# Attention and MLP on one core: the order of products within a group, the maxima of the first block, and the place of two small steps

## The chip, the core and the metric

The kernel runs on one core of one Trainium2 chip. The time is that of the device for one execution in microseconds, and the comparison is between medians of runs on the same chip. Five engines work side by side, each through its own queue in order: TensorE (PE, whose weight loads the profile lists as PEld), VectorE (DVE), ScalarE (ACT), GpSimd (POOL) and SyncE (SP), which here only issues DMA transfers. A transfer, once issued, runs by itself, but SP doesn't issue the next one before the one at the head of its queue has what it waits for.

## What is computed

```
h  = x + softmax((ln(x) wq)(ln(x) wk)^T / 4) (ln(x) wv) wo
h2 = h + silu(ln(h) w1) w2
```

One sequence of S = 2048 rows, D = 512, H = 32 heads of 16, F = 1792, all in float32. `ln` is a layer norm without gain or bias; the softmax runs over all 2048 keys.

## The kernel before

**Projections.** A first part makes the layer norm, the projections for q, k and v, and, beside them, the first row maxima of the scores. float32 products are made of two float16 halves of each operand, so the weights need scale factors. Their sums of squares are gathered on ACT (`square_rest`), reduced in `measure_rest`, and raised to the power -1/2 on POOL; `scale_of` turns each into a power of two on DVE. The factor for the attention output (`norms[:, 3:]`) goes its own way, in `set_output_factors`. Both this and `set_factors` are called when all projections are queued, just before the attention loop.

**Attention.** An item is four heads times a block of 512 queries: 32 items, eight to a block. A group is an item times 128 keys: 16 groups to an item, 512 in all, numbered g through the loop at the end of the kernel. A group has

- four scores (`scores`): a product of 64 rows, `ps<-qs,ks` in the profile, and an exponential on ACT, `pt<-ps`, into one of a ring of tiles;
- n maxima (`one_max`): a product of 48 rows, `ps<-ks,qs`, and a reduction on DVE, `mx<-ps`. They serve a later item: all 64 maxima of an item must be found, and its row maxima placed into `qs`, before its first score. They use a ring of three PSUM banks, so the fourth product waits for the first's reduction;
- the value products (`values`): four, `ps<-pt,va`, one for each head, of float32, in the four column parts of the array. They come at the end of a group and belong to an earlier one: two groups back, or one back where half products run.

Heads come in two kinds, j = 0 and j = 1, whose operands lie in partitions 0 to 63 or 64 to 127. A product of one kind and one of the other run on PE side by side: such a pair is called a slot here. Maxima may be of either kind, so they are chosen to fill the other half.

**Half products.** In 112 groups of each of blocks 1 to 3 (g = 146 to 257, 274 to 385, and from 402 on; the set `beside`) the MLP of the block before runs inside the attention groups. Each of its products, of 128 rows, is cut into two of 64 (`half_product`): an even group makes up to six halves of kind 0, the next, odd one the same six of kind 1, all in PSUM bank 3. To fit, an even group makes the kind 1 scores of itself and of the next group, and the odd one the kind 0 scores of both; so of the value products at the end of an odd group, which belong to the even group before, the second and the fourth use that odd group's first two exponentials. `beside_products` writes the order: a list for the half products' side (`same`) and one for the other (`other`), taken in turns. The first half product of a group gets a wait for an exponential of the group before (`fence`), since the two kinds write into one bank. When all halves of a product are in, `current["end"]` reads the bank on ACT.

**Output groups.** In the first item of blocks 1 to 3 (items 8, 16 and 24), groups c = 9 to 12 of the 16 (g = 137 to 140 in item 8) also multiply 128 finished rows by `wo`: twelve full products, with three maxima in the middle. Their rows then go through layer norm (DVE, POOL), are split in two (`split_normal`: ACT, then POOL or DVE) and turned by a DMA into `hts`, the operand of the first half products (`turn_beside`, `DMA_TRANSPOSE` on SP). These begin at group 146.

**How many maxima.** `maxima(g)` gives n: at most what the ring of `qs` tiles allows, and at least as many as the goals ask for, which are (how many maxima, by which group) for all later items. Groups with half products have four, five while they lag, three where a maximum is placed.

**Placing.** When an item's last maximum is found, `found_maxima` chooses. Far from the item's start (more than `FAR` groups) POOL finishes the maxima, and `CALM` groups later `place_far` turns them on DVE and sends them through DRAM (`md<-mt`, then `qs<-md`, which waits for it on SP). Nearer, `place_max` uses a transpose on PE, a copy on DVE and one transfer (`qs<-mn`).

Of the kernel before, what the change touches and what calls it, by code (L numbers as in the profile page):

```python
# [13 lines left out]
U32 = mybir.dt.uint32  # L14
# [14 lines left out]
NB = S // 512  # L29
# [35 lines left out]
AHEAD = 6  # L65

JOINT = 2
MORE = 3
FAR = 8
CALM = 4  # L70


OUTPUT = 8
# [16 lines left out]
def attention_mlp_kernel(ctx: ExitStack, tc: tile.TileContext, x, wqkv, wo, w1, w2, out):  # L90
# [12 lines left out]
    def pool(op, *a, **k):  # L103
        tc.keep_in_program_order(getattr(nc.gpsimd, op)(*a, **k))  # L104
# [15 lines left out]
    def dve(fn, *a, **k):  # L120
        pin(getattr(nc.vector, fn)(*a, **k))  # L121
# [417 lines left out]
    def scale_of(part, top):  # L539
        dve("tensor_scalar", sigma[:, part], norms[:, part], top, None, op0=ALU.mult)  # L540
        dve("tensor_scalar", sigma[:, part].bitcast(U32), sigma[:, part].bitcast(U32), 0x7F800000, None, op0=ALU.bitwise_and)
        dve("reciprocal", inverse[:, part], sigma[:, part])

    def set_output_factors():
        pool("tensor_scalar", norms[:, 3:], norms[:, 3:], 1e-30, None, op0=ALU.add)
        pool("tensor_tensor", norms[:, 3:], norms[:, 3:], expos[:, 3:], ALU.pow)
        scale_of(slice(3, 4), TOP / BOUND)
        for to, f in ((o_minus, -1.0), (o_twice, 2.0)):
            pool("tensor_scalar", to, o_s, f, None, op0=ALU.mult)

    def set_factors():
        scale_of(slice(3), TOP)
        for to, a, f in ((h_f, inverse[:, :1], 1 / LN), (g_s, w1_s, 1 / 32.0), (g_half, w1_s, 1 / 64.0),
                         (out_f, inverse[:, :1], 32.0)):
# [630 lines left out]
    def beside_products(g, n):  # L1185

        if not current:
            count, share, of, end = chains.pop(0)
            current.update(count=count, share=share, of=of, end=end, half=[0, 0], open=[], gone=0)
        side = g % 2  # L1190
        heads = [(x, k) for x in (g - side, g - side + 1) for k in range(4) if head(x, k)[1] != side]
        i, found, left = next_item(), [0, 0], [0, 0]
        if i < ITEMS:
            left = [len(todo[i, j]) for j in range(2)]
        count = current["count"] - current["half"][0] if side == 0 else current["half"][0] - current["half"][1]
        count = min(current["share"], count)
# [12 lines left out]
        if short > 0:  # L1209
            other[-1:-1] = [("none", 0)] * short  # L1210
        waiting = []
        for m in range(max(len(other), len(same))):
            for kind, x in same[m:m + 1] + other[m:m + 1]:
                if kind == "score":
                    waiting.append(scores(*x))
                    if len(waiting) < 4:
                        waiting[-1]()
# [4 lines left out]
        if current["half"][1] == current["count"]:  # L1222
            current["end"](space[:, 3, :])
            current.clear()
            waiting[3]()
        else:
            current["fence"] = waiting[3]()
# [30 lines left out]
    def finish_last(pending):  # L1258
# [85 lines left out]
        for f in range(FC):  # L1344
# [11 lines left out]
            if f > 1:  # L1356
# [6 lines left out]
    fixed = {**{8 * KC * b + c: 3 + MORE * (OUTPUT < c <= OUTPUT + 4) for b in range(1, NB) for c in range(2, KC + 2)},  # L1363
             **{g: 4 for g in beside}}
    before = [sum(n for x, n in fixed.items() if x < g) for g in range(groups + 1)]
    free = [sum(x not in fixed for x in range(g)) for g in range(groups + 1)]
# [1 line left out]
    def maxima(g):  # L1368
# [9 lines left out]
        goals += [(END - 32 * (1 - a), KC * LAST + HALF * a) for a in range(2) if KC * LAST + HALF * a > g]  # L1378
        rate = 0
        for n, start in goals:  # L1380
            end = max(g + 1, start - AHEAD)
# [4 lines left out]
            rate = min(rate, (ready - at["done"]) / (KC - 1 - c or KC))  # L1386
        at["due"] += rate
        if g < LAG:
            return 0
# [6 lines left out]
    set_output_factors()  # L1396
    set_factors()
    at["attention"] = True
    done = 0
    for g in range(groups):  # L1400
# [108 lines left out]
```

## Time and profile before

| | |
|---|---|
| runs | 1600.78 us median of 3 (1599.69 to 1601.96) |
| profiled execution | 1599.65 us; span 1597.8 us |
| mean granted clock of TensorE | 0.998 |
| PE busy | 1574.8 us (99%) |
| DVE busy | 1375.0 us (86%) |
| ACT busy | 1237.7 us (77%) |
| POOL busy | 565.1 us (35%) |

Times in the profile's rows count from the start of the span. The projections take 177.90 us, the groups before half products begin in block 1 end at 503.09, and the last group with half products ends near 1500. A row of the order of time has start, length, engine, line, operation, what it writes and reads, and a count where like rows are merged; line L97 is the helper through which every product goes, so groups are told apart by tiles. In brackets stands how long the engine was idle before it, and what ended that.

### The profile page before, as it was taken

What the parts mean: (1) busy time and instruction counts of PE and PEld (TensorE: products, weight loads), DVE (VectorE), ACT (ScalarE), POOL (GpSimd) and SP (SyncE); (2) the same over time, 40 slices, a digit from 0 to 9 for tenths busy, and PEclk for the clock granted to TensorE, in tenths of its full rate; (3) what the DMA queues carried; (4) which work ended last, traced back from release to release, by engine and by line L of the source; (5) the groups of instructions that cost most, each with busy time, mean ns of one, the idle gap of its engine ahead of it and who ended that gap; (6) DMA issues with size and microseconds to landing.
All of it is one profiled execution on the core that took longest, in us unless ns stands there. A gap on an engine that the chain in (4) does not pass through costs nothing.

```text
span 1597.8 us, 31074 instructions
## 1 busy us (share of the span) xinstructions
PE 1574.8 (99%) x11495; PEld 474.3 (30%) x11495; DVE 1375.0 (86%) x2211; ACT 1237.7 (77%) x2404; POOL 565.1 (35%) x803
## 2 busy tenths in 40 slices
PE   9999899999999999999999999999999999999999
PEld 6434222222222222222222222222222222222354
DVE  7999899999999999999999999999999999992232
ACT  6545699999987888877778888877768888878632
POOL 6643534544532454312142444310143444211100
PEclk9999999999999999999999999999999999999999
DMA  6667423333333122345433211444333121334332
GB/s 215 174 178 219 133 58 104 96 96 96 91 105 90 41 60 60 93 143 144 119 82 78 59 46 51 123 133 128 108 88 81 50 60 53 88 104 148 115 86 73
DMA packets 134403, 162.39 MB, mean 102 GB/s; under 512 B 41392, under 2 KB 78320, under 8 KB 134252
## 3 DMA queue, kind: packets, MB, share of 16 engines
q1 hardware_dynamic: 129500, 151.89, 34.0%
q10 hardware_dynamic: 4752, 8.52, 1.9%
q8 instruction: 90, 1.47, 0.4%
q14 instruction: 61, 0.50, 0.1%
HBM read 126.61 MB, written 24.76 MB: 95 GB/s over the span
## 4 chain that ended last, share of the span: by engine, by line
PE 90%; DVE 6%; ACT 2%; issue 1%; POOL 1%; POOLq 0%; DVEq 0%; ACTq 0%
PE ps L97 89%; DVE mx L307 3%; ACT pt L111 2%; PE ps L100 1%; DVE mx L305 1%; DVE ot L121 0%; DVE st L121 0%; DVE w L121 0%; DVE pvs L121 0%; POOL wv_l L104 0%; POOL sl L104 0%; DVE ks L121 0%; DVE xtl L121 0%; DVE mv L121 0%; POOL rs L104 0%
## 5 line engine op out<-in xcount | busy, mean ns | idle before, releaser
L307 DVE TENSOR_REDUCE mx<-ps 128x1 f32<-128x512 f32 x1842 | 1145.8, 683 | 87.0 <-PE ps L97 80.3
L111 ACT ACTIVATE pt<-ps 128x512 f32<-128x512 f32 x2048 | 1054.9, 605 | 206.3 <-PE ps L97 200.2
L97 PE MATMUL ps<-qs,ks 64*128 64x512 f16 x2048 | 685.2, 379 | 1.1 <-ACT pt L111 1.0
L97 PE MATMUL ps<-ks,qs 48*128 48x512 f16 x2048 | 628.3, 379 | 13.5 <-DVE mx L307 11.6
L97 PE MATMUL ps<-pt,va 128*17 128x512 f32 x4096 | 542.1, 599 | 1.0 <-DVE pvs L121 0.8
L97 PE MATMUL ps<-hts,w 64*128 64x512 f16 (+2 forms) x1212 | 283.6, 370 | 0.6 <-ACT pt L111 0.6
L97 PE MATMUL ps<-w,gates 64*128 64x512 f16 x1008 | 244.7, 376 | 0.5
L97 PEld LDWEIGHTS <-ks 64*128 64x128 f16 x2048 | 175.1, 94 | 200.2 <-issue 165.3
L97 PEld LDWEIGHTS <-qs 48*128 48x128 f16 x2048 | 146.8, 94 | 293.4 <-issue 281.4
L104 POOL TENSOR_TENSOR ri<-rc,minus 128x16 f32<-128x16 f32 x31 | 90.8, 2928 | 207.8 <-DMA rc<-dn 191.7
L97 PEld LDWEIGHTS <-w 64*128 64x128 f16 (+1 forms) x1212 | 114.0, 94 | 130.2 <-issue 34.5
L97 PEld LDWEIGHTS ps<-pt,va 128*17 128x17 f32 x4096 | 70.4, 95 | 237.5 <-issue 225.4
L97 PEld LDWEIGHTS <-gates 64*128 64x128 f16 x1008 | 92.3, 94 | 130.1 <-issue 28.6
L305 DVE TENSOR_REDUCE mx<-ps 128x2 f32<-128x1024 f32 x103 | 119.2, 1217 | 4.1 <-PE ps L97 3.5
L104 POOL TENSOR_SCALAR t<-t,factors 128x512 f32<-128x512 f32 x42 | 29.2, 695 | 196.9 <-ACT t L111 196.9
L111 ACT ACTIVATE g<-ps,factors 128x512 f32<-128x512 f32 x68 | 47.6, 700 | 42.7 <-PE ps L97 42.6
L104 POOL TENSOR_TENSOR ot<-ot,g 128x512 f32<-128x512 f32 x12 | 15.2, 1266 | 173.9 <-ACT g L111 173.9
L111 ACT ACTIVATE ks<-ps 128x512 f32<-128x512 f32 x30 | 17.9, 598 | 49.9 <-PE ps L97 42.9
L121 DVE SCALAR_TENSOR_TENSOR gh<-g,factors,gh 128x512 f16<-128x512 f32 x14 | 10.5, 751 | 52.1 <-ACT gh L111 52.1
L104 POOL TENSOR_TENSOR t<-t,g 128x512 f32<-128x512 f32 x42 | 53.5, 1275 | 3.5
L104 POOL TENSOR_TENSOR sl<-ks,sh 128x512 f16<-128x512 f32 x30 | 34.7, 1157 | 51.5 <-ACT sh L111 38.3
L104 POOL TENSOR_TENSOR gates<-t,gates 128x512 f16<-128x512 f32 x42 | 48.6, 1158 | 3.4
(161 smaller groups left out, 1019.0 us busy)
## 6 DMA issues: line engine op xcount, KB each, us to landing
w<-w2d SPq DMA_DIRECT2D x182, 256.0 KB
ks<-kd SPq DMA_DIRECT2D x120, 192.0 KB
w<-w1d SPq DMA_DIRECT2D x56, 256.0 KB
ks<-in_B_w_dram ACTq DMA_DIRECT2D x28, 256.0 KB
w<-in_B_w_dram SPq DMA_DIRECT2D x28, 256.0 KB
qs<-qd SPq DMA_DIRECT2D x128, 48.0 KB
kd<-sh SPq DMA_DIRECT2D x16, 256.0 KB
qd<-sh SPq DMA_DIRECT2D x16, 256.0 KB
```

The costliest lines, as they stand in the source:

```text
L97: return tc.keep_in_program_order(nc.tensor.matmul(*a, **k))
L100: tc.keep_in_program_order(nc.tensor.transpose(*a))
L104: tc.keep_in_program_order(getattr(nc.gpsimd, op)(*a, **k))
L111: ins = getattr(nc.scalar, fn)(*a, **k)
L121: pin(getattr(nc.vector, fn)(*a, **k))
L305: pin(nc.vector.tensor_reduce(of, space[:, n:n + 2, :], axis=AX.X, op=ALU.max))
L307: pin(nc.vector.tensor_reduce(of[:, j:j + 1], space[:, n, :], axis=AX.X, op=ALU.max))
```

## The change

Four things change together.

1. `beside_products` puts the half products first and maxima into every other slot of the other side; the fourth maximum comes seventh, beside the last score. The first half product of a group waits for the exponential that follows the last half, which in a full group is the third; before it was the fourth. Where there are few maxima, empty places keep the last score beside the last half.
2. `set_output_factors` is gone: the fourth factor is computed with the other three, and `set_factors` is called before the projection n = 18 of 0 to 19.
3. Of the four output groups only the first two have three more maxima (`MORE` is now a tuple). In the first block, goals beyond item 9 don't count, a group makes three maxima unless four are due, and groups with half products lag by another measure at the end.
4. `FAR` goes from 8 to 5 and `CALM` from 4 to 3, so that more items are placed through DRAM.

```diff
-MORE = 3
-FAR = 8
-CALM = 4
+MORE = 3, 3, 0, 0
+FAR = 5
+CALM = 3
...
-        pool("tensor_scalar", norms[:, :3], norms[:, :3], 1e-30, None, op0=ALU.add)
-        pool("tensor_tensor", norms[:, :3], norms[:, :3], expos[:, :3], ALU.pow)
+        pool("tensor_scalar", norms, norms, 1e-30, None, op0=ALU.add)
+        pool("tensor_tensor", norms, norms, expos, ALU.pow)
...
     def set_factors():
-        scale_of(slice(3), TOP)
+        dve("tensor_scalar", sigma[:, :3], norms[:, :3], TOP, None, op0=ALU.mult)
+        dve("tensor_scalar", sigma[:, 3:], norms[:, 3:], TOP / BOUND, None, op0=ALU.mult)
+        dve("tensor_scalar", sigma.bitcast(U32), sigma.bitcast(U32), 0x7F800000, None, op0=ALU.bitwise_and)
+        dve("reciprocal", inverse, sigma)
...
+            if n == 18:
+                set_factors()
...
-        other = [("max", 1 - side)] * found[1 - side]
-        other = [step for m, of in enumerate(heads) for step in [("score", of), *other[m:m + 1]]]
-        same = [("max", side)] * found[side]
-        same[1:1] = [("half", side)] * count
-        short = len(same) - len(other)
-        if short > 0:
-            other[-1:-1] = [("none", 0)] * short
+        other = [("score", of) for of in heads]
+        for m in range(found[1 - side]):
+            other.insert(2 * m if m < 3 else len(other), ("max", 1 - side))
+        same = [("half", side)] * count + [("max", side)] * found[side]
+        last = max(m for m, step in enumerate(other) if step[0] == "score")
+        if last < count - 1:
+            other[last:last] = [("none", 0)] * (count - 1 - last)
...
+                    if current.get("fence", True) is None:
+                        current["fence"] = weigh()
...
+                    if m == count - 1:
+                        current["fence"] = None
+                        if current["half"][1] == current["count"]:
+                            current["end"](space[:, 3, :])
+                            current.clear()
...
-            weave(project_rows(n, ps), {6: lambda: singles(MORE)})
+            weave(project_rows(n, ps), {6: lambda: singles(MORE[n])})
...
-            most = 4 - late_now + (64 + 4 * (g + LEAD) > at["done"])
+            most = 4 - late_now + (64 + 4 * (g + (LEAD if g < marks[-1] else 3)) > at["done"])
...
-        goals = [(64 * (n + 1), KC * n) for n in range(i + 1, LAST)]
+        goals = [(64 * (n + 1), KC * n) for n in range(i + 1, LAST) if g >= FIRSTS[0] * KC or n <= FIRSTS[0] + 1]
...
-        most = 2 if late_now or c == JOINT and 0 < i <= FIRSTS[0] else 4
+        most = 2 if late_now or c == JOINT and 0 < i <= FIRSTS[0] else 3 + (at["due"] >= 4 and i < FIRSTS[0])
```

**PE, end of group 160 and start of group 161.** In these rows a weight load of `w` opens a half product, of `qs` a maximum, of `ks` a score; `pt,va` are the value products. First the last slots of group 160, before:

```order
L97 LDWEIGHTS w
L97 MATMUL ps<-hts,w 128x512
L97 LDWEIGHTS qs_102
L97 MATMUL ps<-ks_101,qs_102 128x512
L97 LDWEIGHTS w
L97 MATMUL ps<-hts,w 128x512
L97 LDWEIGHTS ks_99
L97 MATMUL ps<-qs_100,ks_99 128x512
L97 MATMUL ps<-pt,va 17x512 x4
```

And now:

```order
L97 LDWEIGHTS w
L97 MATMUL ps<-hts,w 128x512
L97 LDWEIGHTS ks_99
L97 MATMUL ps<-qs_100,ks_99 128x512
L97 LDWEIGHTS qs_102
L97 MATMUL ps<-ks_101,qs_102 128x512
L97 LDWEIGHTS ks_99
L97 MATMUL ps<-qs_100,ks_99 128x512
L97 MATMUL ps<-pt,va 17x512 x4
```

The fourth maximum moved from the sixth slot to the seventh, and the third score took its place. Then the first slots of group 161, before:

```order
L97 LDWEIGHTS qs_102
L97 MATMUL ps<-ks_101,qs_102 128x512
L97 LDWEIGHTS ks_99
L97 MATMUL ps<-qs_100,ks_99 128x512
L97 LDWEIGHTS w
L97 MATMUL ps<-hts,w 128x512
L97 LDWEIGHTS qs_102
L97 MATMUL ps<-ks_101,qs_102 128x512
```

And now:

```order
L97 LDWEIGHTS w
L97 MATMUL ps<-hts,w 128x512
L97 LDWEIGHTS qs_102
L97 MATMUL ps<-ks_101,qs_102 128x512
L97 LDWEIGHTS w
L97 MATMUL ps<-hts,w 128x512
L97 LDWEIGHTS ks_99
L97 MATMUL ps<-qs_100,ks_99 128x512
```

A half product stands in the first slot beside a maximum, and the first score is in the second slot.

**DVE, around the start of the attention.** The ten maxima in the middle are those of the last two projections; the difference of the two orders:

```order
 L121 STREAM_TRANSPOSE mt<-ns 128x32
+L121 TENSOR_SCALAR factors<-norms 128x3
+L121 TENSOR_SCALAR factors<-norms 128x1
+L121 TENSOR_SCALAR factors<-factors 128x4
+L121 RECIPROCAL factors<-factors 128x4
 L307 TENSOR_REDUCE mx<-ps 128x1 x10
-L121 TENSOR_SCALAR factors<-norms 128x1
-L121 TENSOR_SCALAR factors<-factors 128x1
-L121 RECIPROCAL factors<-factors 128x1
-L121 TENSOR_SCALAR factors<-norms 128x3
-L121 TENSOR_SCALAR factors<-factors 128x3
-L121 RECIPROCAL factors<-factors 128x3
```

Four operations stand ahead of these maxima where six stood behind them. POOL's eight small operations on `factors` move with them, from behind the last projection's `sl<-ks,sh` to two projections ahead of it.

**SP, in the output groups of item 8.** The turns of finished rows (`hts<-g`) with what is queued around them, before:

```order
L131 DMA_TRANSPOSE hts<-g 128x8x128
L127 DMA ks_103<-kd 48x2048
L127 DMA w<-w1d 128x1024
L131 DMA_TRANSPOSE hts<-g 128x8x128
L127 DMA w<-w1d 128x1024
L131 DMA_TRANSPOSE hts<-g 128x8x128 x2
L127 DMA w<-w1d 128x1024
```

And now:

```order
L131 DMA_TRANSPOSE hts<-g 128x8x128
L127 DMA md<-mt 32x32 x4
L127 DMA qs_108<-md 2x1024 x2
L127 DMA ks_103<-kd 48x2048
L127 DMA w<-w1d 128x1024
L131 DMA_TRANSPOSE hts<-g 128x8x128
L127 DMA w<-w1d 128x1024
L131 DMA_TRANSPOSE hts<-g 128x8x128 x2
L127 DMA w<-w1d 128x1024
```

The placement of item 9, before a near one (`qs<-mn`, queued ahead of all turns), is a far one and stands between the first turn and the second. In all, 23 placements go through DRAM instead of 13 in the attention loop.

More of the change, by code (lines that the diff above doesn't have):

```diff
@@ L535, in measure_rest @@
         dve("tensor_reduce", norms[:, 2:3], ps[:, 28:n], axis=AX.X, op=ALU.add)
-        pool("tensor_scalar", norms[:, :3], norms[:, :3], 1e-30, None, op0=ALU.add)
-        pool("tensor_tensor", norms[:, :3], norms[:, :3], expos[:, :3], ALU.pow)
[L539 to L549, printed above, removed]
+        pool("tensor_scalar", norms, norms, 1e-30, None, op0=ALU.add)
+        pool("tensor_tensor", norms, norms, expos, ALU.pow)
     def set_factors():
-        scale_of(slice(3), TOP)
+        dve("tensor_scalar", sigma[:, :3], norms[:, :3], TOP, None, op0=ALU.mult)
+        dve("tensor_scalar", sigma[:, 3:], norms[:, 3:], TOP / BOUND, None, op0=ALU.mult)
+        dve("tensor_scalar", sigma.bitcast(U32), sigma.bitcast(U32), 0x7F800000, None, op0=ALU.bitwise_and)
+        dve("reciprocal", inverse, sigma)
         for to, a, f in ((h_f, inverse[:, :1], 1 / LN), (g_s, w1_s, 1 / 32.0), (g_half, w1_s, 1 / 64.0),
-                         (out_f, inverse[:, :1], 32.0)):
+                         (out_f, inverse[:, :1], 32.0), (o_minus, o_s, -1.0), (o_twice, o_s, 2.0)):
             pool("tensor_scalar", to, a, f, None, op0=ALU.mult)
@@ L1214, in beside_products @@
                 if kind == "score":
-                    waiting.append(scores(*x))
-                    if len(waiting) < 4:
-                        waiting[-1]()
+                    weigh = scores(*x)
+                    if current.get("fence", True) is None:
+                        current["fence"] = weigh()
+                    else:
+                        weigh()
                 elif kind == "max":
@@ L1221, in beside_products @@
                     half_product(x)
[L1222 to L1227, printed above, removed]
+                    if m == count - 1:
[3 more added lines that the diff above has]
+                            current.clear()
     found = {}
@@ L1362, in attention_mlp_kernel @@
     beside = {g for m in marks for g in range(m + 2, min(groups, m + 2 + 4 * FC + 4 * FC))}
-    fixed = {**{8 * KC * b + c: 3 + MORE * (OUTPUT < c <= OUTPUT + 4) for b in range(1, NB) for c in range(2, KC + 2)},
+    fixed = {**{8 * KC * b + c: 3 + (MORE[c - OUTPUT - 1] if OUTPUT < c <= OUTPUT + 4 else 0) for b in range(1, NB) for c in range(2, KC + 2)},
              **{g: 4 for g in beside}}
@@ L1374, in maxima @@
             at["due"] = 0
-            most = 4 - late_now + (64 + 4 * (g + LEAD) > at["done"])
+            most = 4 - late_now + (64 + 4 * (g + (LEAD if g < marks[-1] else 3)) > at["done"])
             return max(0, min(most, ready - at["done"]))
-        goals = [(64 * (n + 1), KC * n) for n in range(i + 1, LAST)]
-        goals += [(END - 32 * (1 - a), KC * LAST + HALF * a) for a in range(2) if KC * LAST + HALF * a > g]
+        goals = [(64 * (n + 1), KC * n) for n in range(i + 1, LAST) if g >= FIRSTS[0] * KC or n <= FIRSTS[0] + 1]
+        goals += [(END - 32 * (1 - a), KC * LAST + HALF * a) for a in range(2) if g >= FIRSTS[0] * KC and KC * LAST + HALF * a > g]
         rate = 0
@@ L1388, in maxima @@
         if g < LAG:
+            at["due"] = 0
             return 0
-        most = 2 if late_now or c == JOINT and 0 < i <= FIRSTS[0] else 4
+        most = 2 if late_now or c == JOINT and 0 < i <= FIRSTS[0] else 3 + (at["due"] >= 4 and i < FIRSTS[0])
         n = max(0, min(most, int(at["due"]), ready - at["done"]))
```

3 lines of the change are left out of this document (removed).

## The prediction

> **What bounds the kernel now.** I read the page's busy times, then the chain that ended last, then a table of stretches cut where the program changes its work, and last the order of time inside one group of each kind.
>
> ```profile
> PE 1574.8 (99%) x11495; PEld 474.3 (30%) x11495; DVE 1375.0 (86%) x2211; ACT 1237.7 (77%) x2404; POOL 565.1 (35%) x803
> PE 90%; DVE 6%; ACT 2%; issue 1%; POOL 1%; POOLq 0%; DVEq 0%; ACTq 0%
> ...
> 177.90:193.84 15.94, 11.22 (x65) 1.91 (x65) 10.69 (x23) 9.37 (x18) 10.11 (x20) 0.79 0.75 186
> 503.09:804.71 301.62, 300.92 (x2475) 84.50 (x2472) 278.74 (x455) 252.93 (x490) 101.33 (x154) 1.00 0.33 91
> ```
>
> The columns of the last two are length, then busy time (count) of PE, PEld, DVE, ACT, POOL, granted clock, DMA share, GB/s. They are groups 2 to 5, and the first 112 groups with half products (146 to 257; two more such stretches follow). PE is on the chain for 90%, so a group is worth what passes before PE reaches the next group's first product. In the first stretch PE is busy for 11.22 of 15.94 us at a clock of 0.79; in the other it is never free (300.92 of 301.62), so there the order of its products is all that can change.
>
> **Part 1: the factors move ahead of attention.** DVE, POOL and PE there, then a stretch:
>
> ```profile
> 171.22 6.23 DVE L307 TENSOR_REDUCE mx<-ps 128x1 f32<-128x512 f32 x10
> 181.60 0.15 DVE L121 TENSOR_SCALAR factors<-norms 128x1 f32<-128x1 f32 x1 [4.16 <-POOL norms L104]
> ...
> 179.44 1.16 POOL L104 TENSOR_TENSOR sl<-ks,sh 128x512 f16<-128x512 f32 x1 [2.30 <-issue]
> ...
> 183.81 0.58 PE L97 MATMUL ps<-ks,qs 48*128 48x512 f16 x1 [4.50 <-DVE mx L307]
> 184.31 1.91 PE L97 MATMUL ps<-pt,va 128*17 128x512 f32 x8
> ...
> 183.80:186.10 2.30, 2.29 (x9) 0.15 (x8) 1.74 (x3) 0.00 (x0) 0.34 (x2) 0.50 0.91 196
> ```
>
> DVE's six small operations stand in its queue ahead of the memset and of group 2's maxima, and wait 4.16 us for a power on POOL that stands behind the last projection's subtraction. PE has no free bank for its fourth maximum, idles 4.50 us, and then runs at half clock. In the new order the power is taken with the other three, three projections earlier, and DVE's four operations come ten maxima earlier. Group 2 then goes as fast as its last bank allows. I build it from group lengths below: its products to the fourth score about 1.0 us, the step to the value products 0.3, these 0.98, so 2.3; group 3 waits for late exponentials, 2.4; groups 4 and 5 take 1.96 each: 8.6 instead of 15.94, a gain of 7.3. Against it, four DVE operations of about 0.16 us now stand ahead of ten maxima that run without a gap from 171.22 to 177.45 and pace PE: 0.6 lost. POOL's eight small operations go between subtractions where it idles (2.30 us above). Net **-6.7** (-1.5 if something else fills the gap, -7.3 if the 0.6 is hidden).
>
> [...]
>
> **Part 2: fewer maxima in the first block.** Three groups of three maxima in a row, then one of four with the one behind it:
>
> ```profile
> 231.01:236.89 5.88, 5.88 (x49) 1.32 (x47) 5.61 (x10) 5.88 (x13) 3.48 (x8) 1.00 0.39 112
> 236.89:241.39 4.50, 4.34 (x35) 0.97 (x33) 4.42 (x8) 4.08 (x10) 2.44 (x3) 1.00 0.87 233
> ```
>
> A three costs 1.96; a four costs 4.50 - 2 x 1.96 = 0.58 more, as DVE then paces PE. In groups 6 to 136 the two orders have 28 and 20 fours (twos cost what threes cost): **-4.7** (-4.0 to -5.2).
>
> **Part 3: the third and fourth output group lose three maxima each.** Groups 139 and 140, the pairs 267-268 and 395-396, and group 397:
>
> ```profile
> 479.19:485.77 6.58, 5.67 (x36) 1.57 (x33) 6.16 (x13) 3.08 (x6) 3.02 (x4) 1.00 0.22 60
> 485.77:491.60 5.83, 5.58 (x35) 1.71 (x32) 5.67 (x12) 2.57 (x5) 1.90 (x3) 1.00 0.61 137
> 829.43:841.38 11.95, 10.95 (x65) 3.18 (x62) 11.10 (x22) 5.65 (x11) 4.93 (x7) 1.00 0.48 99
> 1182.78:1193.87 11.09, 10.80 (x64) 3.26 (x61) 10.51 (x21) 5.65 (x11) 4.93 (x7) 1.00 0.01 2
> 1193.87:1197.11 3.24, 2.33 (x20) 0.44 (x17) 3.21 (x8) 2.48 (x5) 0.75 (x2) 1.00 1.00 169
> ```
>
> Without the insert a group is a three (1.96) plus twelve full products at the 0.22 spacing shown below (2.6) plus a mode step, 4.75; DVE's 3.7 us of work hides beside it. Six groups at 4.75 are 28.5 against 12.41 + 11.95 + 11.09 = 35.45, so -6.95; group 138 now has six maxima instead of five, +0.25: **-6.7** (-5 to -8). Group 397 falls from four maxima to three; part of its 3.24 returns in the groups behind it: **-0.8**.
>
> **Part 4: a placement moves into SP's queue ahead of the turns.** SP's last two turns in the output groups, a far placement elsewhere, DVE's work before the place, and a late stretch:
>
> ```profile
> 496.07 2.97 SPq L131 DMA_TRANSPOSE hts<-g  x2
> ...
> 785.74 1.71 SPq L127 DMA_DIRECT2D md<-mt  x4
> 788.52 0.53 SPq L127 DMA_DIRECT2D qs<-md  x2
> ...
> 492.62 0.18 DVE L121 BATCH_NORM_AGGREGATE mv<-st 128x2 f32<-128x6 f32 x1
> ...
> 501.15:503.10 1.95, 1.95 (x21) 0.43 (x17) 1.73 (x4) 1.55 (x4) 0.00 (x0) 1.00 0.15 57
> ```
>
> The far placement is now queued in group 141, behind DVE's 492.8 in old time. SP writes `md` from 493.0, reads it back 2.78 later until 496.3, loads a key block and weights (about 1.1), and only then turns rows 1 to 3: 1.3, a load of 0.6, then 2.6, ending near 501.9 instead of 499.04. Up to now the turned rows had landed by about 501.2 (DMA share 0.15 from there on), 2.2 behind the last issue, and were needed at 503.09, where half products begin. Now they land near 504.0, and the need moves from the second slot to the first: 0.9 late in the first block. In the others groups before that point are slower by some tenths, so I take 0.5 each, **+1.5** (0 to +9). The PE transpose and copy of the old near placement (about 0.4 us of PE and DVE) go from these groups.
>
> **Part 5: groups with half products.** One even group and the next one's first rows, then its fourth maximum's DVE work and exponentials:
>
> ```profile
> 600.59 0.39 PE L97 MATMUL ps<-qs,ks 64*128 64x512 f16 x1
> 601.68 0.38 PE L97 MATMUL ps<-hts,w 64*128 64x512 f16 x1
> 601.76 0.37 PE L97 MATMUL ps<-ks,qs 48*128 48x512 f16 x1
> 601.90 0.38 PE L97 MATMUL ps<-hts,w 64*128 64x512 f16 x1
> 602.28 1.05 PE L97 MATMUL ps<-pt,va 128*17 128x512 f32 x8
> 603.26 0.39 PE L97 MATMUL ps<-ks,qs 48*128 48x512 f16 x1
> ...
> 601.01 0.69 DVE L307 TENSOR_REDUCE mx<-ps 128x1 f32<-128x512 f32 x1 [0.19 <-PE ps L97]
> ...
> 600.39 2.72 ACT L111 ACTIVATE pt<-ps 128x512 f32<-128x512 f32 x5
> 601.54 0.59 ACT L111 ACTIVATE pt<-ps 128x512 f32<-128x512 f32 x1
> ```
>
> The group takes 603.26 - 600.59 = 2.67. In slot five the maximum starts 0.08 behind its partner (601.76 against 601.68): with three banks it waits for the first maximum's reduction, which ended at 601.70. The delay runs on to the last score and the value products behind it. With maxima in slots 0, 2, 4 and 6 the fourth comes 0.22 later, the wait is gone, and an **even** group falls to about 2.60.
>
> In an **odd** group the value products belong to the group before, and two of their four `pt` are this group's first and second exponential. The second ended at 602.13, 1.54 into the group; the value products start at 1.69, so nothing waits. The scores now come one slot (0.23) later. What a wait costs, two groups show:
>
> ```profile
> 545.42 0.60 ACT L111 ACTIVATE pt<-ps 128x512 f32<-128x512 f32 x1
> 546.00 1.10 PE L97 MATMUL ps<-pt,va 128*17 128x512 f32 x8
> 547.04 0.39 PE L97 MATMUL ps<-ks,qs 48*128 48x512 f16 x1
> ...
> 1450.90 1.22 PE L97 MATMUL ps<-pt,va 128*17 128x512 f32 x8
> 1452.07 0.39 PE L97 MATMUL ps<-qs,ks 64*128 64x512 f16 x1
> 1452.50 2.06 ACT L111 ACTIVATE pt<-ps 128x512 f32<-128x512 f32 x4 [0.49 <-PE ps L97]
> 1454.62 0.39 PE L97 MATMUL ps<-qs,ks 64*128 64x512 f16 x1
> 1455.12 1.09 ACT L111 ACTIVATE pt<-ps 128x512 f32<-128x512 f32 x2 [0.55 <-PE ps L97]
> ```
>
> At 545.42 a copy had pushed the second exponential back; it ended at 546.02, the value products took 1.10 instead of 1.05, and the next group came 1.02 behind that end. The second case (1.22; next group 1.17 behind their start instead of 0.98) passes 0.17 of wait on in full. So an odd group takes the second exponential's end plus 1.02. From score to first exponential it is 0.46 in the full groups (a score behind a maximum), and behind a half product 0.43 (1452.07 to 1452.50) or 0.50 (1454.62 to 1455.12; there the group's start itself had waited for an exponential). Such waits for the group's start are hidden now, so I take 0.44, near the lower: end at 1.54 + 0.23 - 0.02 = 1.75, odd group 2.77. A pair costs 5.38 instead of 5.35, over 137 pairs **+4** (+2 at 0.43, +8 at 0.46, +19 at 0.50).
>
> Halves first, and their wait on the **third exponential**: I cost it at nothing. The fourth of the group at 600.59 ended at 603.11, only 0.15 before the next group's first slot; with scores a slot later it would end behind it. The third ends about 0.4 earlier and stays covered; without that cover each group would lose about 0.15. In the 18 remaining groups without maxima the last score still comes with the last half, so they keep the fourth.
>
> What the first block saved must be found later. Three groups of five:
>
> ```profile
> 1210.60:1219.75 9.15, 9.13 (x73) 2.51 (x70) 8.73 (x15) 6.72 (x13) 3.71 (x4) 1.00 0.33 85
> ```
>
> A five costs 3.05, 0.38 over 2.67, in either order, as its last maximum waits for the second's reduction. There are 27 instead of 17: **+3.8**. Four groups fewer run without maxima, +0.4; the 20 odd groups that a copy now delays by 0.05 lose that separate delay, -1.0.
>
> Sum: -6.7 - 4.7 - 6.7 - 0.8 + 1.5 + 4 + 3.8 + 0.4 - 1.0 = **-10.2 us**. The profiled execution took 1599.65 us (span 1597.8), 1.1 below the median 1600.78; I get 1589.5.
>
> **Rivals.**
> *The late second exponential wins (slower).* If the first exponential follows its score by 0.50, an odd group takes 2.83, and an even one 2.66, since its fourth score waits for the bank that this exponential frees. The pair costs 0.14 more, 19 instead of 4: 1604.5. It decides from 0.105 per pair. For it speaks the row at 1455.12, against it that most groups show 0.43 to 0.46. Chance 0.08.
> *The turns arrive late.* SP's queue costs 3 us at each of three starts, +9 instead of +1.5: 1597. For it speaks that `qs` waits for `md` with the turns behind it; against it the 1.9 us between 501.2 and 503.1. Chance 0.10.
> *The gap at the start stays in part*, the accumulator's memset or the late projections' copies on ACT taking over: -1.5 instead of -6.7, 1594.7. Chance 0.10.
> *The stall overlaps the next group.* If the next weights load while the fourth value product waits, 0.09 of each odd group's stall is hidden: 12 less, 1577.5. The case at 1450.90, which passed all on, speaks against it. Chance 0.08.
> [...]
>
> **How the numbers follow.** The forecast with its small terms (1585 to 1594) has 0.56, the four rivals 0.36, and 0.08 is left to mixtures. A change of 0.2% (3.2 us) is about what a measurement can tell. Faster: 0.56 + 0.08 + 0.10, half of the turns' 0.10, most of the rest: 0.84; same 0.07; slower 0.09. The range 1581 to 1598 takes in the forecast, the start's rival and half of the turns'.
>
> **What would show it.** Right: no PE idle time near 180 and a clock of 1.00 there; even groups near 2.60, odd near 2.77 with value products of about 1.2; output groups 139 and 140 near 4.75. Wrong: odd groups above 2.8; a wait of PE for `hts` at the first half product; a four that costs nothing once neighbours change.

## The result: 13.5 us slower, and the profile after

| | before | after |
|---|---|---|
| runs | 1600.26 us median of 4 (1599.69 to 1601.96) | 1613.72 us median of 4 (1612.78 to 1615.9) |
| ratio | | 1.0084, 95% interval 1.0067 to 1.0102 |
| span of the profiled execution | 1597.8 us | 1612.1 us |
| mean granted clock | 0.998 | 0.993 |

The forecast was 1589.5 (1581 to 1598), so it has the wrong sign. Busy times and the chain that ended last, on the page of after:

```profile
PE 1586.0 (98%) x11485; PEld 520.1 (32%) x11485; DVE 1377.2 (85%) x2199; ACT 1240.0 (77%) x2404; POOL 577.8 (36%) x861
PE 88%; DVE 8%; ACT 1%; DMA 1%; issue 1%; POOL 0%; SPq 0%; POOLq 0%; ACTq 0%; DVEq 0%
```

PE is busy 11 us longer for ten products fewer. Behind the stalls products ran at a lower clock (0.50 in groups 144, 272 and 400; 8 us more in the five groups of the table), and in groups with half products a value product that waits for its exponential counts as busy (1.22 us for the four at 705.71 below, 1.05 at 484.73; 12 us more there; elsewhere it is 9 less). With both traces cut at the starts of the same groups, each part of the change has its own stretch:

| stretch | before | after | difference | predicted |
|---|---|---|---|---|
| up to group 2 | 177.90 | 179.42 | +1.5 | +0.6 |
| groups 2 to 5 | 15.94 | 8.63 | -7.3 | -7.3 |
| groups 6 to 136 | 274.57 | 269.45 | -5.1 | -4.7 |
| output groups, three times four | 68.27 | 61.08 | -7.2 | -6.7 |
| **the five groups behind them, three times** | 36.38 | 55.25 | **+18.9** | +0.7 |
| groups with half products and to 510 | 902.2 | 916.0 | **+13.7** | +7.2 |
| groups 258 to 264 and 386 to 392, end | 122.5 | 122.3 | -0.2 | 0 |

The differences add up to +14.3, which is the difference of the spans. The stretches of after, in the columns of the prediction's first table (length, busy PE, PEld, DVE, ACT, POOL, granted clock, DMA share, GB/s): groups 2 to 5, group 139, groups 141 and 142, then 143, 144 and 145 by themselves, and the first 112 groups with half products:

```profile
179.42:188.05 8.63, 8.53 (x61) 1.88 (x62) 7.30 (x13) 8.43 (x18) 1.16 (x1) 1.00 0.60 141
468.38:473.12 4.74, 4.71 (x32) 1.61 (x29) 3.96 (x8) 3.08 (x6) 2.74 (x5) 1.00 0.01 3
477.86:482.48 4.62, 4.61 (x34) 0.87 (x30) 4.58 (x9) 4.20 (x9) 1.90 (x3) 1.00 0.02 2
482.48:488.27 5.79, 3.15 (x20) 0.61 (x17) 2.19 (x4) 1.50 (x4) 0.00 (x0) 1.00 0.88 216
488.27:493.07 4.80, 4.55 (x16) 0.57 (x16) 3.76 (x7) 3.66 (x7) 0.00 (x0) 0.50 0.50 110
493.07:495.95 2.88, 2.88 (x19) 0.59 (x16) 1.89 (x3) 2.06 (x4) 0.00 (x0) 0.65 0.00 0
495.95:805.24 309.29, 307.82 (x2486) 101.59 (x2483) 285.01 (x465) 253.66 (x488) 101.70 (x154) 1.00 0.32 89
```

The first two rows are as forecast: the gap at the start is closed at full clock, and an output group without maxima takes 4.74. The stall sits in group 143, where PE is busy 3.15 of 5.79 us; groups 144 and 145 then run at a clock of 0.50 and 0.65. What PE waited for is found by going back one engine at a time. PE and ACT in the order of time (start, length; in brackets the idle time before and what ended it):

```profile
480.71 2.10 ACT L111 ACTIVATE pt<-ps 128x512 f32<-128x512 f32 x4
484.73 1.05 PE L97 MATMUL ps<-pt,va 128*17 128x512 f32 x8
487.10 0.62 ACT L111 CAST g<-w 128x512 f16<-128x512 f32 x1 [4.29 <-DMA hts<-g]
488.27 0.58 PE L97 MATMUL ps<-qs,ks 64*128 64x512 f16 x1 [2.49 <-ACT pt L111]
```

PE waits for an exponential to free a score bank. ACT isn't short of scores. At the head of its queue stands the split of the last finished row (`g<-w`), and that waits 4.29 us for a turn (`hts<-g`) to end, because there are two buffers `g` and the turn reads the one that is wanted. SP's queue shows why the turn is late (two of the placement's four writes stand ahead of these rows):

```profile
480.02 0.88 SPq L127 DMA_DIRECT2D md<-mt  x2
482.04 0.52 SPq L127 DMA_DIRECT2D qs<-md  x2
482.60 0.31 SPq L127 DMA_DIRECT2D ks<-kd  x1
482.95 0.43 SPq L127 DMA_DIRECT2D w<-w1d  x1
483.42 1.25 SPq L131 DMA_TRANSPOSE hts<-g  x1
485.40 4.31 SPq L131 DMA_TRANSPOSE hts<-g  x2
```

The turn at 483.42 is row 1's. It stands behind the far placement and its reading back, and it is this turn that frees the buffer. One odd group with half products (from 704.04; the score, the first two exponentials, the value products, the next group), and the even group and the odd one as stretches:

```profile
704.27 0.38 PE L97 MATMUL ps<-qs,ks 64*128 64x512 f16 x1
704.76 1.08 ACT L111 ACTIVATE pt<-ps 128x512 f32<-128x512 f32 x2 [0.60 <-PE ps L97]
705.71 1.22 PE L97 MATMUL ps<-pt,va 128*17 128x512 f32 x8
706.86 0.39 PE L97 MATMUL ps<-w,gates 64*128 64x512 f16 x1
701.43:704.04 2.61, 2.61 (x23) 0.84 (x22) 2.28 (x5) 1.96 (x4) 0.00 (x0) 1.00 0.22 63
704.04:706.86 2.82, 2.82 (x26) 0.96 (x24) 2.69 (x5) 2.18 (x5) 0.00 (x0) 1.00 0.92 251
```

The second exponential ends at 705.84, and the next group comes 1.02 later, as forecast. But the first one starts 0.49 behind its score, not 0.44.

### The profile page after: what moved, and what is told of

It reads as the page before. It is cut to its first block, busy times and chain, and to the rows that moved or that the text cites. A ratio compares the mean times of both kernels' runs of the same rounds, so it can differ in the third digit from the quotient of the medians.

```text
span 1612.1 us, 31239 instructions
## 1 busy us (share of the span) xinstructions
PE 1586.0 (98%) x11485; PEld 520.1 (32%) x11485; DVE 1377.2 (85%) x2199; ACT 1240.0 (77%) x2404; POOL 577.8 (36%) x861
## 4 chain that ended last, share of the span: by engine, by line
PE 88%; DVE 8%; ACT 1%; DMA 1%; issue 1%; POOL 0%; SPq 0%; POOLq 0%; ACTq 0%; DVEq 0%
PE ps L97 87%; DVE mx L307 6%; DVE mx L305 1%; PE ps L100 1%; ACT pt L111 1%; DMA hts<-g 1%; ACT g L111 0%; POOL wv_l L104 0%; DMA w<-w2d 0%; SPq L127 0%; DVE pvs L121 0%; DVE g L121 0%; DVE st L121 0%; DVE ot L121 0%; DVE ks L121 0%
## 5 line engine op out<-in xcount | busy, mean ns | idle before, releaser
L97 PE MATMUL ps<-ks,qs 48*128 48x512 f16 x2048 | 680.4, 382 | 7.6 <-DVE mx L307 4.0
L97 PE MATMUL ps<-qs,ks 64*128 64x512 f16 x2048 | 644.4, 380 | 11.8 <-ACT pt L111 11.7
L97 PE MATMUL ps<-pt,va 128*17 128x512 f32 x4096 | 565.5, 601 | 0.5 <-DVE pvs L121 0.3
L97 PEld LDWEIGHTS <-qs 48*128 48x128 f16 x2048 | 169.2, 95 | 78.3 <-issue 35.3
L97 PEld LDWEIGHTS <-w 64*128 64x128 f16 (+1 forms) x1212 | 102.0, 95 | 236.8 <-ACT pt L111 105.6
L97 PEld LDWEIGHTS ps<-pt,va 128*17 128x17 f32 x4096 | 84.5, 95 | 221.3 <-issue 207.5
L97 PEld LDWEIGHTS <-gates 64*128 64x128 f16 x1008 | 82.1, 94 | 218.4 <-ACT pt L111 119.7
L104 POOL TENSOR_TENSOR mx<-mx 128x32 f32<-128x32 f32 x52 | 12.4, 239 | 109.2 <-DVE mx L307 102.6
```

What stands on the lines that cost most here:

```text
L97: return tc.keep_in_program_order(nc.tensor.matmul(*a, **k))
```

## Experiments

Medians are given beside those of the kernel before in the same comparison (1600.4 to 1601.1 us). "The five groups" are 141 to 145, 269 to 273 and 397 to 401.

### The stall: three buffers g

```diff
-zp.tile([P, 512], F32, name="g")
+zp.tile([P, 512], F32, name="g", bufs=3)
```

> The changed kernel with three buffers g instead of two, nothing else; SP's order stays as it is. Theory: ScalarE's 4.3 us wait for the buffer goes and with it the half clock, but the second to fourth turn still stand behind the far placement, so the first half products (group 146 and its like) may wait up to 2 us for turned rows: 4 to 6 us less in each of three blocks, 1596 to 1602 us. Rival 1: what stops the groups is SP's queue itself (the row maxima qs arrive late): ScalarE's wait goes, TensorE's stall stays, 1611 to 1614 us. Rival 2: the turned rows are covered after all: 1594 us, the same as with the near placement.

Measured: 1598.14 us, ratio 0.9985 (0.9975 to 0.9995). ACT no longer waits for a turn. The five groups as stretches, then two pieces of the chain in the third block:

```profile
477.64:490.43 12.79, 12.12 (x79) 2.35 (x76) 12.34 (x21) 11.33 (x23) 1.90 (x3) 1.00 0.56 139
833.91:846.47 12.56, 11.55 (x79) 2.22 (x76) 11.45 (x21) 11.50 (x23) 2.21 (x3) 1.00 0.60 138
1190.46:1203.77 13.31, 11.54 (x79) 2.21 (x76) 11.45 (x21) 11.50 (x23) 2.22 (x3) 1.00 0.64 136
...
1197.91 5.08 DMA hts<-g
1202.98 0.79 issue
```

16.6 us of the 18.9 are gone, and the clock stays at 1.00, though SP's order is the same. So the buffer is the cause, and the first rival (late `qs`) falls. What is left in the third block is the wait that the prediction had in mind: PE's first half product waits 1.76 us for a turn that lands at 1202.98. In the first block it waits 0.51 for an exponential instead, as it does with the new order alone (below). In the second it waits 1.00, and a turn and a copy on ACT end at nearly the same time (846.34 and 846.42).

### The same stall: the near placement

```diff
-FAR = 5
+FAR = 6
```

> The changed kernel with FAR at 6 instead of 5: only the items 9, 17 and 25, whose maxima are complete six groups ahead, are placed by the near way again. Theory: in the changed kernel the far placement holds back the second turn in SP's queue; the buffer g of that row (there are two) stays occupied, ScalarE waits 4.3 us for it with the exponentials of two groups behind, and TensorE idles and then runs at half clock. With the near placement that wait goes: groups 141 to 145 and their like take 11.5 to 12.7 us instead of 18.1 to 18.9, together 17 to 19 us less, against about 1 us for transposes and copies: about 1596 us. Rival: the stall comes from the output groups having lost their maxima, which brings the rows' layer norm and splits too close together: then the stall stays, 1612 to 1614 us.

Measured: 1603.28 us, ratio 1.0018 (1.0008 to 1.0028): 7 us more than expected. In the first block ACT waits less, but still waits. Its waits between 478 and 493 us (total, count, longest), the five groups, then two parts of them:

```profile
ACT g L111 <- DMA hts<-g: 1.0, 1, 1.0
478.00:492.88 14.88, 13.56 (x80) 2.66 (x77) 11.36 (x20) 11.24 (x22) 1.90 (x3) 0.89 0.64 137
484.00:488.00 4.00, 2.75 (x15) 0.57 (x15) 2.71 (x5) 3.36 (x7) 0.00 (x0) 1.00 0.66 157
488.36:491.90 3.54, 3.54 (x20) 0.67 (x23) 2.47 (x6) 2.11 (x5) 0.00 (x0) 0.54 0.31 81
```

So placement alone isn't the whole cause: the output groups are shorter now, and the last row asks for its buffer about 1 us early even without a placement in the way. Then the clock falls to 0.54, though no single wait of PE is above 0.8 us, and the block loses 3.4 us in all. The rival, which would have left all of the stall, is wrong too.

### Both, with the old order

FAR at 6, three buffers `g`, and `beside_products` as before (the next section).

> The changed kernel with FAR at 6, the order of before in groups with half products, and three buffers g. Theory: with the near placement ScalarE still waits 0.5 to 1 us for a buffer g, since the output groups without maxima follow one another 1.1 us faster than the turns free it; with a third buffer groups 141 to 145 and their like take about 12 us each, as in the kernel before, instead of 14.3, 14.4 and 12.7: 5 us less than 1590.6, about 1585.5 us. Rival: the turned rows, whose order on SP is unchanged, are then what the first half products wait for: 1588 us or more.

Measured: 1584.62 us, ratio 0.9896 (0.988 to 0.9913). The five groups:

```profile
478.03:489.53 11.50, 11.48 (x80) 2.23 (x77) 10.97 (x20) 10.50 (x22) 2.12 (x3) 1.00 0.78 177
829.92:841.41 11.49, 11.47 (x79) 2.23 (x76) 10.96 (x20) 10.49 (x22) 2.12 (x3) 1.00 0.91 179
1181.80:1193.29 11.49, 11.47 (x79) 2.22 (x75) 10.96 (x20) 10.49 (x22) 2.13 (x3) 1.00 0.84 179
```

No wait is left: 11.5 us in every block, where the kernel before took 11.49, 12.22 and 12.67.

### The far placement alone, in the kernel before

```diff
-FAR = 8
-CALM = 4
+FAR = 5
+CALM = 3
```

> The kernel before with FAR at 5 and CALM at 3 alone, so that 28 placements go through DRAM, those of the items 9, 17 and 25 among them, in output groups that still carry their twelve maxima. It also has 5 instead of 17 groups of five maxima, worth 4.5 us. Theory: ScalarE's stall needs both parts of the change, the far placement in SP's queue and output groups 1.1 to 1.8 us shorter, which ask for the third buffer g sooner. Here the second turn is issued before the last row is split, so the stall stays away and at most the last turns are late: groups 141 to 145 and their like cost 0 to 1.5 us more each time, 1596 to 1600 us in all. Rival: the far placement alone brings the stall: 1612 us or more.

Measured: 1601.66 us, ratio 1.0007 (0.9997 to 1.0016), between the two. The five groups, then SP in the third block, in the second and in the first:

```profile
491.67:503.16 11.49, 11.47 (x79) 2.23 (x76) 10.97 (x20) 10.50 (x22) 2.13 (x3) 1.00 0.55 126
840.92:854.44 13.52, 12.14 (x79) 2.46 (x75) 10.96 (x20) 10.71 (x22) 1.90 (x3) 1.00 0.76 174
1192.67:1210.37 17.70, 14.93 (x79) 2.61 (x76) 12.43 (x21) 11.33 (x22) 1.90 (x3) 0.81 0.49 102
...
1186.41 1.30 SPq L131 DMA_TRANSPOSE hts<-g  x1
1194.00 1.72 SPq L127 DMA_DIRECT2D md<-mt  x4
1198.16 1.25 SPq L131 DMA_TRANSPOSE hts<-g  x1
...
836.44 1.70 SPq L127 DMA_DIRECT2D md<-mt  x4
841.28 1.30 SPq L131 DMA_TRANSPOSE hts<-g  x1
843.71 1.25 SPq L131 DMA_TRANSPOSE hts<-g  x1
...
481.48 2.64 SPq L127 DMA_DIRECT2D md<-mt  x4
487.01 1.37 SPq L131 DMA_TRANSPOSE hts<-g  x1
490.20 1.25 SPq L131 DMA_TRANSPOSE hts<-g  x1
```

The theory's condition was wrong: long output groups don't protect. In the third block the placement stands between the first turn and the second, and the stall is there (+5.0 over the kernel before). In the second and the first it stands ahead of both; that costs 1.3 in the second and nothing in the first. What goes with the cost is how late the second turn is issued: 5.5 and 2.8 us into the five groups, and 1.5 ahead of them.

### The new order alone, in the kernel before

Only `beside_products` is exchanged.

> The kernel before with the new order in groups with half products alone. Theory: even groups 2.61 instead of 2.675, odd groups 2.82 (2.75 in about a quarter of them) instead of 2.675, so 137 pairs cost 0.07 more each, with 17 groups of five at 0.03 more: 10 us more, 1610 us. Rival: the loss in the changed kernel comes from its placements through DRAM (DVE's transposes, SP's queue) and not from the order: within 3 us of before.

Measured: 1610.74 us, ratio 1.0059 (1.0043 to 1.0076), as expected. Even groups take 2.61, odd ones 2.82. The five groups cost 0.58 more in each block. PE's first half product now opens group 146, and there it waits 0.5 us for the last exponential of group 145, in all three blocks; in the kernel before it stood a slot later and waited 0.19 in the first block, as the first of these rows shows (the second is of this run). The turned rows have nothing to do with it.

```profile
503.67 0.37 PE L97 MATMUL ps<-hts,w 64*128 64x512 f16 x1 [0.19 <-ACT pt L111]
...
504.11 0.37 PE L97 MATMUL ps<-hts,w 64*128 64x512 f16 x1 [0.51 <-ACT pt L111]
```

### The old order in the changed kernel

FAR at 6, and `beside_products` as before.

> The changed kernel with FAR at 6 and, in groups with half products, the order of before (scores first, fence on the fourth exponential). It shows what the new order alone is worth, against the run with FAR at 6. Theory: the new order gains 0.06 in an even group and loses 0.07 to 0.14 in an odd one (2.61 and 2.75 to 2.82 us, against 2.675 twice), so the old order is 5 to 10 us faster: 1587 to 1591 us when the other run takes 1596. Rival: groups of one kind lose in the one order what they gain in the other, since DVE and ScalarE set the pair: within 2 us of the run with FAR at 6.

Measured: 1590.57 us, ratio 0.9938 (0.9921 to 0.9954), against 1603.28 with the new order. In the groups with half products up to 485 the old order saves 3.5, 3.6 and 2.2 us, 9.3 in all; the rest lies in the five groups.

### The score first in odd groups

FAR at 6 and the new order, with this in odd groups (and the wait on DVE's reduction where that follows the last half):

```diff
-            other.insert(2 * m if m < 3 else len(other), ("max", 1 - side))
+            other.insert(2 * m + side if m < 3 else len(other), ("max", 1 - side))
```

> The changed kernel with FAR at 6; in odd groups with half products the score takes the first slot of the other side and maxima the second, fourth and sixth, while even groups keep the new order. The first half product of the next group waits for the reduction in the sixth slot where that is the first work of another engine behind the last half. Theory: an odd group takes the end of its second exponential plus 1.02; with the first score a slot earlier that end falls from 1.80 to about 1.57, so seven slots and the value products set its length, 2.61 to 2.66 us instead of 2.75 to 2.82: 137 times 0.13 to 0.18, 18 to 25 us less than with FAR at 6 alone, about 1573 us. Rival: the fourth exponential, now a slot nearer the end in relation to the even group's first, or the fourth maximum's bank takes over and the odd group stays at 2.68 or more: 1583 us or more.

Measured: 1594.05 us, ratio 0.9958 (0.9942 to 0.9975), 21 us over the theory. The second exponential is early now (1.58 into the group), but an odd group still takes 2.73. In one that starts at 698.36, the first reduction and the fourth maximum's product:

```profile
699.04 0.69 DVE L307 TENSOR_REDUCE mx<-ps 128x1 f32<-128x512 f32 x1 [0.37 <-PE ps L97]
699.78 0.37 PE L97 MATMUL ps<-ks,qs 48*128 48x512 f16 x1
```

The fourth maximum waits until 699.73, when the first one's bank is free: there are three. With the first maximum a slot later the seventh slot is too early. That is the rival's bank. Maxima in slots 0, 2, 4 and 6 are thus what the new order gains by, and the late score is what it pays.

### A mixture

FAR at 6, three buffers, the new order (behind the `if`) only in even groups of fewer than five maxima, elsewhere that of before.

```diff
+        if side == 0 and sum(found) < 5:
...
+        else:
...
```

> The changed kernel with FAR at 6, three buffers g, and two orders in groups with half products: even groups with fewer than five maxima keep the new one, odd groups and those of five take that of before. Theory: an even group takes 2.61 us by the new order and 2.67 by the old, an odd one 2.82 and 2.67; what the order of one kind is worth doesn't depend on the other's, so 137 even groups save 0.06 each, 8.4 us less than with the old order in both: about 1577 us. Rival: the even group's late fourth exponential, which in the new order ends 0.11 behind the next group's start, pushes the odd group's first exponential back and makes the odd group 2.73 as the other mixture did: about 1585 us, no better than the old order in both.

Measured: 1578.04 us, ratio 0.9856 (0.984 to 0.9873). Even groups take 2.61 and odd ones 2.675, so what the order is worth in one kind doesn't depend on the other. This beats both kernels.

### The factors

In the kernel before, their move alone:

> The kernel before with the factors' move alone. Theory: groups 2 to 5 take 8.6 us instead of 15.9 and the last projections 1.3 to 1.5 us more, and nothing later depends on it: 5.8 us less, 1594.5 us. Rival: the four groups' gain is given back by later groups, which wait for the maxima or for DVE's memset: 1598 us or more.

Measured: 1595.53 us, ratio 0.9966 (0.9953 to 0.9978). By medians that is 5.6 less, near the 5.8 expected; by stretches of the two traces it is 4.2, as groups 2 to 5 take 9.96 and start at 179.69. In the changed kernel the same stretch takes 8.63, 1.33 less: its new rules for maxima leave thirteen DVE operations in these groups, where there are seventeen here. (The start differs too, 179.42, but the eight traces with these projections start group 2 anywhere from 179.08 to 179.48.) In the mixture, two other places for `set_factors`:

```diff
-            if n == 18:
-                set_factors()
...
-    BESIDE_T = {6: lambda: begin_scores(3), 11
+    BESIDE_T = {6: lambda: (begin_scores(3), set_factors()), 11
```

> The kernel of the mixture (near placement, three buffers g, new order in even groups) with the factors computed behind the first three maxima of the projection n = 18, instead of ahead of them. Theory: ahead of them DVE's first factor operation meets GpSimd's subtraction and takes 1.00 us instead of 0.15, so that four operations cost 1.5 us of DVE's time, which paces the last projections; three maxima later GpSimd is idle and they cost 0.6: group 2 starts at 178.4 us instead of 179.3. Rival: the four operations cost 1.5 us wherever they stand among the maxima: 179.3.

```diff
-(begin_scores(2), singles(2))}
+(begin_scores(2), singles(2), set_factors())}
```

> The same with the factors behind all ten maxima, where DVE has nothing to do before the accumulator's memset. Theory: the maxima are not delayed, so group 2 starts at 177.9 as in the kernel before; the power is long done, so DVE waits for nothing, and groups 2 to 5 take 8.6 to 9.0 us: 1.0 to 1.4 us less in all than the mixture. Rival: GpSimd's subtraction of that projection stands in the way of DVE's first operation again, the memset and the maxima of group 2 come 0.5 to 1 us later, and groups 2 to 5 take 9.5 us or more.

Measured: group 2 starts at 178.72 and 178.10 instead of 179.29, and groups 2 to 5 take 8.63 in both (1576.8 and 1576.38 us, one execution each, against 1578.04 in another comparison, whose kernel before was 0.5 slower). DVE's first factor operation with GpSimd's subtraction in after, then the same operation in the first of these:

```profile
171.36 1.16 POOL L104 TENSOR_TENSOR sl<-ks,sh 128x512 f16<-128x512 f32 x1 [2.43 <-ACT sh L111]
171.55 1.00 DVE L121 TENSOR_SCALAR factors<-norms 128x3 f32<-128x3 f32 x1
...
173.48 0.16 DVE L121 TENSOR_SCALAR factors<-norms 128x3 f32<-128x3 f32 x1
```

Three elements for each partition take 1.00 us beside the subtraction and 0.16 without it.

### Maxima in all four output groups

```diff
-MORE = 3, 3, 0, 0
+MORE = 3, 3, 3, 3
```

> The mixture with three maxima in each of the four output groups, as in the kernel before. 14 groups of five maxima are left of 29. Theory: without another wait an output group with maxima takes 5.38 us, as the undisturbed ones of before did, against 4.74: six times 0.64, 3.9 us more; 15 fives become fours, 0.38 to 0.44 each, 5.7 to 6.6 less: about 2 us less than the mixture, 1576 us. So taking these maxima out gained nothing by itself. Rival: the output groups' old 5.7 to 6.6 us come back, since layer norm and maxima meet on DVE: 3 us or more above the mixture, 1581 us.

Measured: 1580.71 us, ratio 0.9876 (0.986 to 0.9893), 2.7 over the mixture, so the rival's sign. Output groups cost 1.62 more in each block and the five groups 0.72, 7.0 in all instead of 3.9; the half-product groups take 2.4 and 2.4 less in the first two blocks and 0.6 more in the third, so fewer fives save 4.1 instead of about 6. In the changed kernel's setting, taking these maxima out gains about 3 us.

## Why the prediction was wrong, by its own steps

- **Part 1** (-6.7): -5.8. The gap went as built from group lengths, 8.63 against 8.6. The 0.6 lost to DVE was 1.5, since the price of 0.16 came from a row without GpSimd's subtraction beside it; the two other places of the factors show this. The term also credited the factors with 1.3 us that the new rules for maxima bring.
- **Part 2** (-4.7): -5.1. **Part 3** (-6.7): -7.2, with 4.74 for the output groups where 4.75 was built. Group 397 lost its fourth maximum as foretold (it takes 1.96), but the groups behind it lost more than it gained; with near placement, three buffers and the old order these five groups take 11.49 instead of 12.67, so the term (-0.8) was -1.2.
- **Part 4** (+1.5) is the step that failed: the five groups cost +18.9, where +0.7 was forecast with group 397's gain. It did see the placement go ahead of the turns in SP's queue, and the rival of late turns priced it at 3 us a start. Both followed the delay only to the **reader of the turned rows**, the first half products. With three buffers the five groups lose 1.3, 1.1 and 1.8 us (against 11.5), 4.2 in all. Of each, 0.6 is what the new order costs there by itself, and only in the third block is PE seen to wait for a turn alone. So that path is small, and within the 0 to 9 given. Not followed was the **buffer that the turn reads**: `g` has two, its next writer is on ACT, and eight exponentials stand behind it. This is shown by the third buffer, which takes 16.6 us away with SP's order kept. The output groups' gain (Part 3) brought the writer forward: with near placement, two buffers and the new order the five groups take 14.87, 14.46 and 14.88 us behind the shorter output groups, and 12.07, 12.79 and 13.25 behind the longer ones of before.
- The half clock, which the kernel before has at the start (0.50 behind a wait of 4.50 us), came here instead: group 144 and its like ran at it behind each stall (0.50), and about half of 145 or more (0.65, 0.77 and 0.76 on average).
- **Part 5** (+7.2): +13.7. The formula (second exponential's end plus 1.02) held in each kind of group (1.02 in 136 of the 138 below). Mis-sized was one number: from score to first exponential it is 0.42 in 35, 0.48 in 84 and 0.51 in 19 of the 138 odd groups with four maxima, so these take 2.75, 2.82 and 2.84 (two of the last kind 3.43), where 0.44 and 2.77 were assumed. The two orders differ by 9.3 us instead of 4. The rival of the late exponential had the mechanism at 0.50, and 0.08 as its chance; even groups, which it also put up, came out at 2.61. The fives and the groups without maxima cost 4.2, as forecast (near placement, three buffers and old order against the kernel before, groups 146 on); in the new order a five takes 3.09, not 3.05 "in either order". That 20 odd groups would lose a delay (-1.0) was half right: 19 of them are the ones at 2.84, 0.02 above the others instead of 0.05.
- What separates the 0.42 from the 0.48 stands in the trace of after. In the 35, the operation just ahead on ACT is the MLP's (`t<-g`), and the exponential waits for one semaphore. In the other 103, ACT runs a semaphore instruction of its own first (0.02 us), and the exponential waits for two. The new order alone shows the same split in all its 139 such groups, and the kernel before has the second wait in none. The prediction's two rows were already such a pair: the exponential at 1452.50 (0.43) has one wait, that at 1455.12 (0.50) two. It put the difference down to the group's start, and took the value near the lower. (By its own formula the pairs cost 2.7 at 0.43 and 6.9 at 0.46, where it says 2 and 8; the sum uses neither.)
- *Start gap stays*: didn't happen. *Stall overlaps*: didn't happen; waits were passed on in full (the 1.02 above).

The terms for the start, the first block and the output groups held to within 0.9 us each; two misjudged waits, 18 and 6.5 us, turned the sign.

What stays open: why the new order gives most of these exponentials their second wait. By the trace ACT itself raises that semaphore; no run takes the wait away and leaves the rest as it is.

## What to carry to other kernels

When a transfer is moved back in a queue, follow both of its ends: who reads what it writes, and who next writes what it reads. Here a ring of two buffers turned a late reader into a stall of ACT, which fills the ring (4.29 us in the first block), with eight exponentials queued behind it. And the gain ahead of the ring used up its slack (behind the shorter output groups ACT waited 1.0 us even with the near placement), so the same edit may want one more buffer; here a third one together with the better half of each edit made 1578 us out of 1614.

## What the runs showed of the hardware

- **Half clock without a long idle time.** With the near placement PE was busy 2.75 of the 4.00 us before 488, never idle for more than 0.8 at a time, and then ran at 0.54 for 3.5 us; in the changed kernel a wait of 2.49 was followed by 4.80 us at 0.50. In the clock records of the kernel before (once) and of the changed one (three times), but for the last few us of each, half clock lasts 6.83 us each time; with the near placement it was about 3.4 (1.00 up to 488, 0.66 up to 490, 0.50 up to 492 and 0.99 up to 494, from which I estimate 488.6 to 492.0). The share of busy time alone doesn't sort these cases: with three buffers PE was busy for 1.65 of the 3.41 us from 1200.96, all but the wait of 1.76, and the clock stayed at 1.00 (the mean of that run is 1.0).
- **A small DVE operation that lasted until GpSimd's had ended.** In after, the operation on three elements began at 171.55 and ended at 172.55, GpSimd's subtraction ran from 171.36 to 172.52: 1.00 us beside it, where the same operation took 0.16 behind the first three maxima, with no operation of GpSimd beside it. Why, no run shows.
